# A decode block on one core: x stationary in the q projection and FFN up, h turned on VectorE, and other pieces for the last load

## The chip, the cores and the metric

The kernel runs on one core of one Trainium2 chip. The metric is the device time of one execution in microseconds (us). The kernel before took 122.86 us (median of 3 runs, 122.75 to 123.06). The engines carry their names in the profile: PE is TensorE's matmuls, PEld its weight loads, DVE is VectorE, ACT is ScalarE, POOL is GpSimd, and SP is SyncE, which issues the DMAs.

## The reference, cut to what matters

Eight tokens (one per batch entry) go through a layer norm. Then 32 query heads attend over the last 1,024 entries of a cache with 8 KV heads, a gated FFN runs beside it, and the two are multiplied.

```python
xn = _layernorm(x)                                   # x: [8, 1, 512], bf16
q  = xn @ wq                                         # wq: [512, 4096]
k, v = k_cache[:, :, Sk-W:, :], v_cache[:, :, Sk-W:, :]   # [8, 8, 1024, 128] each, W = 1024
s  = softmax(q k^T * Dh**-0.5) v, heads joined, @ wo # wo: [4096, 512]
g  = silu((gelu(xn @ w_gate) * (xn @ w_up)) @ w_down)# [512, 1792], [512, 1792], [1792, 512]
out = x + s * g
```

Only eight rows of x meet every weight, so the work is mostly loading: 47.5 MB of weights and cache are read once.

## The kernel before

Everything is loaded by one queue (SP) in a fixed order, into a ring of ten buffers: wq, then K and V for 16 units of work, then the FFN weights, then wo in four pieces.

```python
wq_t = [load_rows(A_wq, KD, k, 2, "wq_t") for k in (0, 2)]
# ... cut: layer norm, constants, the loop over 16 units that loads K and V ...
wg_t = load_rows(B_w_gate, KD, 0, KD, "wg_t")
wu_t = load_rows(B_w_up, KD, 0, KD, "wu_t")
load_cache(A_v_cache, NU - 1, v_t, "v_t")
wd_t = load_rows(B_w_down, FJ, 0, FJ, "wd_t")
wo_t = [[load_rows(A_wo[: HT * Dh, :], WI, 0, WI, "wo_t")]]          # first half, 16 rows per partition
wo_t.append([load_rows(A_wo[HT * Dh :, :], WI, 0, 8, "wo_t")])       # second half: 8 rows ...
nc.sync.dma_start(out=xr[0:P:4, :], in_=...)                         # x once more, 8 KB
wo_t[1].append(load_rows(A_wo[HT * Dh :, :], WI, 8, 5, "wo_t"))      # ... 5 rows ...
wo_t[1].append(load_rows(A_wo[HT * Dh :, :], WI, 13, 3, "wo_t"))     # ... and 3 rows
```

In the q projection and in FFN up, the weights are the stationary operand (the one that is loaded into the matmul array first: for q the trace has 128 loads of 128x128, 104 ns each, beside the 128 matmuls) and the eight columns of x move past them:

```python
for h in range(Hq):                       # 32 heads x 4 = 128 matmuls of 8 columns
    for k in range(KD):
        nc.tensor.matmul(qT_ps[:, h, :], wq_t[k // 2][:, k % 2, h * Dh : (h + 1) * Dh],
                         xnT[:, k, :], start=(k == 0), stop=(k == KD - 1))
# ... cut ...
for w, wt in enumerate((wg_t, wu_t)):     # 2 x 14 x 4 = 112 matmuls of 8 columns
    for j in range(FJ):
        for k in range(KD):
            nc.tensor.matmul(gu_ps[:, w, j, :], wt[:, k, :].rearrange("p (m j) -> p j m", j=FJ)[:, j, :],
                             xnT[:, k, :], start=(k == 0), stop=(k == KD - 1))
# ... cut: GELU on [128, 14, 8]; the product lands as hT, already turned ...
```

The end of the kernel multiplies wo in the order in which its pieces land, four column tiles (quarters of the array, 32 columns each) at a time, then two VectorE operations and the store follow:

```python
for t in range(NT):
    i = 0
    for w in wo_t[t]:
        for r in range(w.shape[1]):
            for q in range(NQ):
                nc.tensor.matmul(s_ps[32 * q : 32 * (q + 1), :], oR[:, t, i, :], w[:, r, q * NW : (q + 1) * NW],
                                 start=(t == 0 and i == 0), stop=(t == NT - 1 and i == WI - 1),
                                 tile_position=(0, 32 * q))
            i += 1
nc.vector.tensor_tensor(out=tmp, in0=s_ps, in1=g_sb, op=ALU.mult)
nc.vector.tensor_tensor(out=out_sb, in0=tmp, in1=xr, op=ALU.add)
```

The softmax here doesn't subtract the row's maximum and nothing guards it: scores larger than these inputs give would overflow.

Of the kernel before, what the change touches and what calls it, by code (L numbers as in the profile page):

```python
# [7 lines left out]
ACT = mybir.ActivationFunctionType  # L8
ALU = mybir.AluOpType
AX = mybir.AxisListType  # L10
BF16 = mybir.dt.bfloat16
FP32 = mybir.dt.float32
# [5 lines left out]
def kernel(  # L18
# [13 lines left out]
    nc = tc.nc  # L32

    B, Sq, D = A_x.shape
    Hkv, Sk, Dh = A_k_cache.shape[1], A_k_cache.shape[2], A_k_cache.shape[3]
    Hq = A_wq.shape[1] // Dh
# [3 lines left out]
    F = B_w_gate.shape[1]  # L40
    P = nc.NUM_PARTITIONS
    KD = D // P
    FJ = F // P
    CS = 4
    NH = Hkv // CS
    HS = CS * rep
# [4 lines left out]
    CC = 2 * HS  # L51
    NQ = 4
    NW = D // NQ
    NT = 2
    HT = Hq // NT
    WI = HT * Dh // P
# [6 lines left out]
    pad = ctx.enter_context(tc.tile_pool(name="pad", bufs=1))  # L63
    ring = ctx.enter_context(tc.tile_pool(name="ring", bufs=10))
    consts = ctx.enter_context(tc.tile_pool(name="consts", bufs=1))
    kT_pool = ctx.enter_context(tc.tile_pool(name="kT_pool", bufs=8))
    p_pool = ctx.enter_context(tc.tile_pool(name="p_pool", bufs=3))
    small = ctx.enter_context(tc.tile_pool(name="small", bufs=2))
    ps_k = ctx.enter_context(tc.tile_pool(name="ps_k", bufs=3, space=bass.MemoryType.PSUM))
    ps_s = ctx.enter_context(tc.tile_pool(name="ps_s", bufs=2, space=bass.MemoryType.PSUM))  # L70
    ps_p = ctx.enter_context(tc.tile_pool(name="ps_p", bufs=1, space=bass.MemoryType.PSUM))
# [5 lines left out]
    def bank(pool, name, shape, dtype=FP32):  # L77
        return pool.tile(shape, dtype, name=name, tag=pool.name)
# [9 lines left out]
    def load_rows(src, rows, r0, n, name):  # L88

        t = ring.tile([P, n, src.shape[1]], BF16, name=name, tag="slot")  # L90
        nc.sync.dma_start(out=t, in_=src.rearrange("(p r) n -> p r n", r=rows)[:, r0 : r0 + n, :])  # L91
        return t
# [3 lines left out]
    def load_cache(cache, u, slots, name):  # L96
# [10 lines left out]
    wq_t = [load_rows(A_wq, KD, k, 2, "wq_t") for k in (0, 2)]  # L107
# [4 lines left out]
    ident = consts.tile([P, P], BF16, name="ident")  # L112
    nc.vector.memset(ident, 0.0)
    nc.gpsimd.affine_select(
        out=ident, in_=ident, compare_op=ALU.not_equal, fill=1.0,
# [15 lines left out]
        out=xhat, in0=x_sb, scalar1=mv[:, 0:1], scalar2=rstd[:, 0:1],  # L131
        op0=ALU.subtract, op1=ALU.mult,
    )
    xnT = consts.tile([P, KD, B], BF16, name="xnT")
    xnT_ps = bank(ps_o, "xnT_ps", [P, KD, B], BF16)
    for k in range(KD):
        nc.tensor.transpose(
# [1 line left out]
            xhat.rearrange("b (p k) -> b k p", k=KD)[:, k, :],  # L139
            ident[0:B, 0:B],  # L140
        )
    nc.vector.tensor_copy(out=xnT, in_=xnT_ps)


    sel4 = consts.tile([P, CS], FP32, name="sel4")
# [1 line left out]
        out=sel4, in_=ident.rearrange("p (a n) -> p n a", n=CS), axis=AX.X, op=ALU.add  # L147
# [24 lines left out]
    identf = consts.tile([P, P], FP32, name="identf")  # L172
    nc.vector.tensor_copy(out=identf, in_=ident)

    perm = consts.tile([P, 2, 2, Dh // 2], BF16, name="perm")
    nc.vector.tensor_copy(
        out=perm,
        in_=ident.rearrange("p (i r) -> p r i", r=2).unsqueeze(2).to_broadcast([P, 2, 2, Dh // 2]),
    )

    own2 = consts.tile([P, 2], FP32, name="own2")
    nc.vector.tensor_reduce(
        out=own2, in_=ident.rearrange("p (g c n) -> p c g n", c=2, n=HS), axis=AX.XY, op=ALU.add
# [5 lines left out]
        in_=ident.rearrange("p (a n) -> p n a", n=HS), axis=AX.X, op=ALU.add,  # L189
    )  # L190

    Q2 = consts.tile([P, 2, B, NH, 2, HS], BF16, name="Q2")
    nc.vector.memset(Q2, 0.0)
    ownm = consts.tile([P, HT, WM], BF16, name="ownm")
    nc.vector.tensor_copy(out=ownm, in_=own16.unsqueeze(2).to_broadcast([P, HT, WM]))
    hT = consts.tile([P, FJ, 32], BF16, name="hT")
    nc.vector.memset(hT, 0.0)
    oR = consts.tile([P, NT, WI, 32], BF16, name="oR")
    nc.gpsimd.memset(oR, 0.0)


    qT = consts.tile([P, B, Hq], BF16, name="qT")
    qT_ps = bank(ps_s, "qT_ps", [P, Hq, B])
    for h in range(Hq):
        for k in range(KD):
            nc.tensor.matmul(  # L206
                qT_ps[:, h, :],
                wq_t[k // 2][:, k % 2, h * Dh : (h + 1) * Dh],
                xnT[:, k, :],
                start=(k == 0),  # L210
                stop=(k == KD - 1),
            )
    nc.vector.tensor_copy(out=qT, in_=qT_ps.rearrange("p h b -> p b h"))  # L213
    qp_ps = bank(ps_s, "qp_ps", [P, 2, B * NH, HS])
    for r in range(2):
        nc.tensor.matmul(
            qp_ps[:, r, :, :].rearrange("p a n -> p (a n)"),
            perm[:, r, :, :].rearrange("p c i -> p (c i)"),
            qT.rearrange("p b h -> p (b h)"),
            start=True, stop=True,  # L220
        )
    for c in range(2):
        p0 = c * (P // 2)
        nc.vector.tensor_copy(
            out=Q2[p0 : p0 + P // 2].rearrange("p r b h c n -> p r (b h) c n")[:, :, :, c, :],
            in_=qp_ps[p0 : p0 + P // 2],
        )


# [18 lines left out]
    def scores(u):  # L248
        h, b = divmod(u, B)
        sc_ps = bank(ps_s, "sc_ps", [P, NPC * P])  # L250
        nc.tensor.matmul(  # L251
            sc_ps, maskL.rearrange("p a n j -> p (a n j)"), maskR.rearrange("p a n -> p (a n)"),
            start=True, stop=False, skip_group_check=True,
        )
        for r in range(2):
            for g in range(NG):
                nc.tensor.matmul(  # L257
                    sc_ps[CC * g : CC * (g + 1), :],
                    Q2[:, r, b, h, :, :].rearrange("p c n -> p (c n)"),
                    kTs[u, g][:, :, r],  # L260
                    start=False, stop=(r == 1), tile_position=(0, CC * g),
                    skip_group_check=True,
                )
        ps[u] = p_pool.tile([P, NPC, P], BF16, name="p_sb")
        xs[u] = p_pool.tile([P, 2 * Dh + 1], FP32, name="x_u")
        nc.scalar.activation(  # L266
            out=ps[u].rearrange("p c s -> p (c s)"), in_=sc_ps, func=ACT.Exp, scale=inv_sqrt_dh,
            accum_out=xs[u][:, 2 * Dh : 2 * Dh + 1],
        )
# [97 lines left out]
    nc.sync.dma_start(  # L367
        out=xr[0:P:4, :], in_=x_flat.rearrange("b (q n) -> q b n", n=NW)
    )
    wo_t[1].append(load_rows(A_wo[HT * Dh :, :], WI, 8, 5, "wo_t"))  # L370
    wo_t[1].append(load_rows(A_wo[HT * Dh :, :], WI, 13, 3, "wo_t"))
    gather(NU - 3)
    turn(NU - 2)
    scores(NU - 1)
    values(NU - 2)


    gu_ps = bank(ps_s, "gu_ps", [P, 2, FJ, B])
    for w, wt in enumerate((wg_t, wu_t)):
        for j in range(FJ):  # L380
            for k in range(KD):
                nc.tensor.matmul(  # L382
                    gu_ps[:, w, j, :],
                    wt[:, k, :].rearrange("p (m j) -> p j m", j=FJ)[:, j, :],
                    xnT[:, k, :],
                    start=(k == 0),
                    stop=(k == KD - 1),
                )
    zT = gu_ps[:, 0, :, :]
    uT = gu_ps[:, 1, :, :]  # L390
    z2 = consts.tile([P, FJ, B], FP32, name="z2")
    nc.scalar.activation(out=z2, in_=zT, func=ACT.Square)  # L392
    nc.vector.tensor_scalar(  # L393
        out=z2, in0=z2, scalar1=0.044715, scalar2=1.0, op0=ALU.mult, op1=ALU.add
    )
    u3 = consts.tile([P, FJ, B], FP32, name="u3")
    nc.vector.tensor_tensor(out=u3, in0=z2, in1=zT, op=ALU.mult)
    th = consts.tile([P, FJ, B], FP32, name="th")
    nc.scalar.activation(out=th, in_=u3, func=ACT.Tanh, scale=0.7978845608028654)
    nc.vector.tensor_scalar(  # L400
        out=th, in0=th, scalar1=0.5, scalar2=0.5, op0=ALU.mult, op1=ALU.add
    )
    nc.vector.tensor_tensor(out=u3, in0=th, in1=zT, op=ALU.mult)
    nc.vector.tensor_tensor(out=hT[:, :, 0:32:4], in0=u3, in1=uT, op=ALU.mult)

    gather(NU - 2)
    turn(NU - 1)
# [25 lines left out]
    for t in range(NT):  # L433
        i = 0
# [47 lines left out]
```

## Time and profile before

| What | Value | View |
|---|---|---|
| time | 122.86 us (span of the profiled run 120.8) | times, page |
| DMA share of the 16 engines, 3 to 105 us | 1.01, at 426 to 429 GB/s | windows |
| PE, DVE, ACT busy | 78%, 52%, 20% of the span | page |
| last piece of wo landed | 116.61 us | landing records |

The first fence shows lines of the profile's page for the kernel before: span, busy time of each engine with its count of instructions, then two rows of the picture in 40 slices (one digit is tenths of a slice of 3 us), then the DMA queues (packets, MB, share of 16 engines), and last the shares of the chain that ended last.

```profile
span 120.8 us, 2828 instructions
PE 93.8 (78%) x1214; PEld 65.2 (54%) x1214; DVE 63.2 (52%) x125; ACT 24.1 (20%) x54; POOL 1.4 (1%) x6
...
PEclk9999999999999999999999967999999965555555
DMA  3999999999999999999999999999999999999700
...
q1 hardware_dynamic: 5976, 47.47, 93.4%
q8 instruction: 9, 0.15, 0.4%
q14 instruction: 3, 0.02, 0.0%
...
DMA 67%; PE 22%; DVE 4%; SPq 2%; issue 1%
```

The DMA row is full from the second slice to slice 37. The PE row is high too, but the chain names DMA. The windows view of the same kernel tells it in numbers (columns: stretch, length, busy time of each engine with its instructions, granted PE clock, DMA share, GB/s):

```profile
3.00:40.00 37.00, 26.06 (x329) 19.74 (x329) 20.34 (x46) 6.67 (x14) 0.00 (x0) 1.00 1.01 426
40.00:80.00 40.00, 36.09 (x383) 22.45 (x382) 26.58 (x45) 9.60 (x23) 0.00 (x0) 0.96 1.01 426
80.00:105.00 25.00, 23.36 (x297) 17.05 (x299) 11.03 (x22) 6.24 (x15) 0.00 (x0) 0.86 1.01 429
105.00:113.00 8.00, 6.15 (x162) 4.51 (x158) 3.80 (x8) 0.28 (x1) 0.00 (x0) 0.50 0.98 413
113.00:116.00 3.00, 1.63 (x52) 1.24 (x45) 0.00 (x0) 0.00 (x0) 0.00 (x0) 0.50 0.43 166
```

The stream never pauses until 113 us (share 0.98 to 1.01). Then the last three microseconds move little: DMA share 0.43. So a faster compute phase in the middle cannot help, and the question is what happens after 113 us. The timeline of the kernel before shows the phases that the change touches and the end (columns: start and length in us, engine, line, operation, output and input, count, and in brackets how long the engine was idle just before it and what ended that):

```profile
94.57 3.52 PE L382 MATMUL gu_ps<-xnT,wg_t 128*128 128x8 bf16 x56
98.97 3.52 PE L382 MATMUL gu_ps<-xnT,wu_t 128*128 128x8 bf16 x56 [0.87 <-DMA wu_t<-in_B_w_up_dram]
...
110.80 1.90 PE L438 MATMUL s_ps<-wo_t,oR 128*32 128x128 bf16 x64
112.86 1.04 PE L438 MATMUL s_ps<-wo_t,oR 128*32 128x128 bf16 x32 [0.16 <-DMA wo_t<-in_A_wo_dram]
114.40 0.72 PE L438 MATMUL s_ps<-wo_t,oR 128*32 128x128 bf16 x20 [0.50 <-DMA wo_t<-in_A_wo_dram]
116.66 0.51 PE L438 MATMUL s_ps<-wo_t,oR 128*32 128x128 bf16 x12 [1.53 <-DMA wo_t<-in_A_wo_dram]
117.22 0.29 DVE L446 TENSOR_TENSOR tmp<-s_ps,g_sb 128x128 f32<-128x128 f32 x1 [5.47 <-PE s_ps L438]
117.67 0.29 DVE L448 TENSOR_TENSOR out_sb<-tmp,xr 128x128 bf16<-128x128 f32 x1 [0.16 <-DVE tmp L446]
117.99 0.62 SPq L449 DMA_DIRECT2D out_dram<-out_sb  x1
```

PE waits 1.53 us for the last three rows of wo, 384 KB, which at 426 GB/s are 0.9 us of stream. Something holds that piece. The trace also records each increment of a DMA's semaphore. For the last piece of wo in the kernel before these are (us):

```
113.51 113.60 113.75 113.79 113.81 113.86 | 114.24 | 114.84 114.94 115.07 115.11 115.15 115.19 115.22 115.25 | 116.61
```

There are 16 increments, as many as the page counts DMA engines, and the matmuls start at 116.66, 0.05 us after the last of them and 1.41 us after the fifteenth. I take each increment as one engine that has landed its share. That is a reading of the counts: the records don't name the engine. On that reading six engines were done by 113.86, 2.75 us before the last one, and fifteen by 115.25, 1.36 us before it.

What held the others is in the third part of the page: queues of kind "instruction". The trace's packet records give their times in the kernel before (16 KB packets took 0.88 to 0.97 us, 8 KB packets 0.31 to 0.34 us):

```
16 KB (q8):  18.73  32.71  43.29  57.00  69.44  82.95  96.91  104.22  114.32
8 KB (q14):  40.70  85.77  118.32
```

Set beside the landings, each of them shows. In the DMA that ended after the first one, one engine landed 1.3 us after the other fifteen (21.49 against 20.17 us). After two, two engines were late (36.12 and 36.38; the next 34.91). After the 8 KB packet at 40.70 three, after the one at 43.29 four, and by 75.5 us six, after six packets. The delay stayed: after the first packet one engine was again last by 1.31 us at 23.92, by 1.26 us at 26.35 and by 1.24 us at 31.22. A stream in which every engine has its equal share to bring and no pause to catch up (DMA share 1.01 from 3 to 105 us) would fit. At the end there are nine late engines and one slightly late one, ten for the ten packets up to 104.22. The eleventh, at 114.32, made no tenth late engine. It made one that was already late land another 1.36 us later, alone at 116.61. After it, the last four packets of that engine start at 115.27 and end at 116.21, when all the other engines had ended by 114.97.

### The profile page before, as it was taken

Reading aid. Unit: us, or ns where it says so; the run is one execution under the profiler, and the core shown is the slowest. Engines: PE = TensorE matmul, PEld = TensorE weight load, DVE = VectorE, ACT = ScalarE, POOL = GpSimd, SP = SyncE. Lnnn points to the kernel's source line nnn. Section 1 sums busy time; section 2 is a strip of 40 time slices with the busy share of each in tenths; the row PEclk is TensorE's granted clock in tenths of the full one; section 3 lists DMA queues with packets and bytes.
Section 4 is the critical chain, followed back from the end, with each engine's and each line's share of the span. In section 5 each row is a group of like instructions: output and inputs, shape, how many; then the busy total and the mean of one; then the engine's idle time right before and its main releaser. Section 6 shows DMA issues by size and latency. Waiting matters only on the chain.

```text
span 120.8 us, 2828 instructions
## 1 busy us (share of the span) xinstructions
PE 93.8 (78%) x1214; PEld 65.2 (54%) x1214; DVE 63.2 (52%) x125; ACT 24.1 (20%) x54; POOL 1.4 (1%) x6
## 2 busy tenths in 40 slices
PE   0000789999987989889889399999999979786720
PEld 0000779666655655565556266666666869365610
DVE  3750039687745757458557964677676100457010
ACT  4500000241232212412133012412413300300000
POOL 4000000000000000000000000000000000000000
PEclk9999999999999999999999967999999965555555
DMA  3999999999999999999999999999999999999700
GB/s 100 434 434 426 415 428 423 428 420 428 428 420 426 428 420 426 428 426 423 423 434 423 434 412 428 426 428 426 423 453 422 420 418 444 429 423 409 320 6 5
DMA packets 6004, 47.65 MB, mean 394 GB/s; under 512 B 736, under 2 KB 744, under 8 KB 1000
## 3 DMA queue, kind: packets, MB, share of 16 engines
q1 hardware_dynamic: 5976, 47.47, 93.4%
q8 instruction: 9, 0.15, 0.4%
q14 instruction: 3, 0.02, 0.0%
q10 hardware_dynamic: 16, 0.01, 0.0%
HBM read 47.46 MB, written 0.01 MB: 393 GB/s over the span
## 4 chain that ended last, share of the span: by engine, by line
DMA 67%; PE 22%; DVE 4%; SPq 2%; issue 1%
DMA k_t<-in_A_k_cache_dram 49%; DMA wo_t<-in_A_wo_dram 18%; PE kT_ps L240 10%; PE tot L298 3%; PE sc_ps L257 3%; PE x_ps L283 3%; DVE kT L242 2%; SPq L100 2%; PE sc_ps L251 1%; PE pT_ps L274 1%; SPq L91 1%; DVE o_sb L315 1%; PE s_ps L438 0%; PE r_ps L333 0%; DVE e L322 0%
## 5 line engine op out<-in xcount | busy, mean ns | idle before, releaser
L242 DVE COPY kT<-kT_ps 128x1024 bf16<-128x1024 bf16 x64 | 42.6, 688 | 23.1 <-PE kT_ps L240 21.8
L240 PE MATMUL kT_ps<-identf,k_t 128*128 128x128 f32 x256 | 40.4, 298 | 3.0 <-DMA k_t<-in_A_k_cache_dram 3.0
L240 PEld LDWEIGHTS kT_ps<-identf,k_t 128*128 128x128 f32 x256 | 30.2, 150 | 14.1 <-issue 9.8
L266 ACT ACTIVATE p_sb<-sc_ps 128x512 bf16<-128x512 f32 x16 | 9.6, 597 | 39.6 <-PE sc_ps L257 26.0
L276 ACT COPY pT<-pT_ps 128x512 bf16<-128x512 bf16 x16 | 9.4, 586 | 31.0 <-PE pT_ps L274 31.0
L298 PE MATMUL tot<-x_u,zsel 128*128 128x257 f32 x32 | 12.2, 467 | 2.6 <-DVE x_u L289 2.4
L283 PE MATMUL x_ps<-v_t,pT 128*32 128x256 bf16 x256 | 10.4, 284 | 0.7 <-ACT pT L276 0.7
L257 PE MATMUL sc_ps<-kT,Q 128*32 128x512 bf16 x128 | 10.6, 407 | 0.0
L206 PE MATMUL qT_ps<-xnT,wq_t 128*128 128x8 bf16 x128 | 3.7, 168 | 8.2 <-DMA wq_t<-in_A_wq_dram 8.2
L298 PEld LDWEIGHTS tot<-x_u,zsel 128*128 128x128 f32 x32 | 5.2, 204 | 6.3 <-DVE x_u L289 6.3
L289 DVE TENSOR_TENSOR x_u<-x_ps,own 128x256 f32<-128x256 f32 x16 | 6.8, 422 | 2.8 <-PE x_ps L283 2.8
L206 PEld LDWEIGHTS <-wq_t 128*128 128x128 bf16 x128 | 3.6, 104 | 8.4 <-DMA wq_t<-in_A_wq_dram 8.4
L283 PEld LDWEIGHTS <-pT 128*32 128x32 bf16 x256 | 5.5, 98 | 4.2 <-issue 2.2
L251 PE MATMUL sc_ps<-maskR,maskL 128*128 128x512 bf16 x16 | 6.5, 405 | 0.0
L274 PE MATMUL pT_ps<-ident,p_sb 128*128 128x128 bf16 x64 | 6.4, 225 | 0.0
L274 PEld LDWEIGHTS <-p_sb 128*128 128x128 bf16 x64 | 5.0, 101 | 2.3 <-issue 0.3
L438 PE MATMUL s_ps<-wo_t,oR 128*32 128x128 bf16 x128 | 4.2, 310 | 2.2 <-DMA wo_t<-in_A_wo_dram 2.2
L257 PEld LDWEIGHTS <-Q 128*32 128x32 bf16 x128 | 1.9, 95 | 5.5 <-issue 5.5
L213 DVE CAST qT<-qT_ps 128x256 bf16<-128x256 f32 x1 | 0.4, 424 | 8.5 <-PE qT_ps L206 8.5
L438 PEld LDWEIGHTS <-oR 128*32 128x32 bf16 x128 | 3.3, 140 | 2.8 <-issue 2.8
L393 DVE TENSOR_SCALAR z<-z 128x112 f32<-128x112 f32 x1 | 0.2, 219 | 7.6 <-ACT z L392 7.6
L382 PE MATMUL gu_ps<-xnT,wu_t 128*128 128x8 bf16 x56 | 3.5, 202 | 0.9 <-DMA wu_t<-in_B_w_up_dram 0.9
(62 smaller groups left out, 42.6 us busy)
## 6 DMA issues: line engine op xcount, KB each, us to landing
k_t<-in_A_k_cache_dram SPq DMA_DIRECT2D x16, 1024.0 KB, 19.6
v_t<-in_A_v_cache_dram SPq DMA_DIRECT2D x16, 1024.0 KB, 19.7
wq_t<-in_A_wq_dram SPq DMA_DIRECT2D x2, 2048.0 KB, 9.4
wo_t<-in_A_wo_dram SPq DMA_DIRECT2D x1, 2048.0 KB, 27.4
wg_t<-in_B_w_gate_dram SPq DMA_DIRECT2D x1, 1792.0 KB, 21.4
wu_t<-in_B_w_up_dram SPq DMA_DIRECT2D x1, 1792.0 KB
wd_t<-in_B_w_down_dram SPq DMA_DIRECT2D x1, 1792.0 KB, 25.0
wo_t<-in_A_wo_dram SPq DMA_DIRECT2D x1, 1024.0 KB, 27.3
```

Of the source, the lines that this page charges most:

```text
L206: nc.tensor.matmul(qT_ps[:, h, :], wq_t[k // 2][:, k % 2, h * Dh : (h + 1) * Dh], xnT[:, k, :], start=(k == 0), stop=(k == KD - 1),)
L240: nc.tensor.transpose(kT_ps[:, pc, :], k32[:, w * P : (w + 1) * P], identf)
L242: nc.vector.tensor_copy(out=kT.rearrange("p s r -> p (s r)"), in_=kT_ps.rearrange("p c s -> p (c s)").bitcast(BF16),)
L251: nc.tensor.matmul(sc_ps, maskL.rearrange("p a n j -> p (a n j)"), maskR.rearrange("p a n -> p (a n)"), start=True, stop=False, skip_group ...
L257: nc.tensor.matmul(sc_ps[CC * g : CC * (g + 1), :], Q2[:, r, b, h, :, :].rearrange("p c n -> p (c n)"), kTs[u, g][:, :, r], start=False, s ...
L266: nc.scalar.activation(out=ps[u].rearrange("p c s -> p (c s)"), in_=sc_ps, func=ACT.Exp, scale=inv_sqrt_dh, accum_out=xs[u][:, 2 * Dh : 2 ...
L274: nc.tensor.transpose(pT_ps[:, pc, :], ps[u][:, pc, :], ident)
L276: nc.scalar.copy(out=pTs[u], in_=pT_ps)
L283: nc.tensor.matmul(x_ps[CC * g : CC * (g + 1), :, :].rearrange("p c d -> p (c d)"), pTs[u][:, pc, CC * g : CC * (g + 1)], v_t[u // 2][:, u ...
L289: nc.vector.tensor_tensor(out=xs[u][:, 0 : 2 * Dh].rearrange("p (c d) -> p c d", d=Dh), in0=x_ps, in1=own2.unsqueeze(2).to_broadcast([P, 2 ...
L298: nc.tensor.matmul(tot[h], zsel[:, B - 1 - b : P + B - 1 - b], xs[u], start=(b == 0), stop=(b == B - 1),)
L438: nc.tensor.matmul(s_ps[32 * q : 32 * (q + 1), :], oR[:, t, i, :], w[:, r, q * NW : (q + 1) * NW], start=(t == 0 and i == 0), stop=(t == N ...
```

## The change

The intent: PE does fewer and longer matmuls in the q projection and in FFN up (x, spread over 32 columns, is now the operand that is loaded, into each of four column tiles, and the weights move past it, up to 512 columns at once); the gate gets its own tile so that GELU can start before w_up lands; and the last load is cut smaller, so that less work is left when it lands. The price: q and h come out in rows and have to be turned, q by 16 small matmuls, h by one 32x32-block transpose on VectorE. Two of eight kT buffers are given up for the room.

```diff
-    kT_pool = ctx.enter_context(tc.tile_pool(name="kT_pool", bufs=8))
+    kT_pool = ctx.enter_context(tc.tile_pool(name="kT_pool", bufs=6))
...
+    xnT = consts.tile([P, KD, 32], BF16, name="xnT")
+    nc.vector.memset(xnT, 0.0)
...
-    for h in range(Hq):
-        for k in range(KD):
+    q_ps = [bank(ps_s, "q_ps", [P, HQ // 2, Dh]) for _ in range(2)]
+    for k in range(KD):
+        for s in range(2):
+            for t in range(NQ):
+                c0 = (t * HQ + s * HQ // 2) * Dh
+                nc.tensor.matmul(
+                    q_ps[s][32 * t : 32 * (t + 1), :, :].rearrange("p n d -> p (n d)"),
+                    xnT[:, k, :],
+                    wq_t[k // 2][:, k % 2, c0 : c0 + HQ // 2 * Dh],
+                    start=(k == 0), stop=(k == KD - 1), tile_position=(0, 32 * t),
+                )
... (four copies to q_row, then 16 matmuls with the identity turn q; Q2 is laid out with the batch innermost)
-    wo_t[1].append(load_rows(A_wo[HT * Dh :, :], WI, 8, 5, "wo_t"))
-    wo_t[1].append(load_rows(A_wo[HT * Dh :, :], WI, 13, 3, "wo_t"))
+    wo_t[1].append(load_rows(A_wo[HT * Dh :, :], WI, 8, 4, "wo_t"))
+    wo_t[1].append(load_rows(A_wo[HT * Dh :, :], WI, 12, 3, "wo_t"))
+    wo_t[1].append(load_rows(A_wo[HT * Dh :, :], WI, 15, 1, "wo_t"))
...
+    gu_ps = [bank(ps_s, "gu_ps", [P, FW]) for _ in range(2)]
     for w, wt in enumerate((wg_t, wu_t)):
-        for j in range(FJ):
-            for k in range(KD):
+        for k in range(KD):
+            for q in range(NQ):
                 nc.tensor.matmul(
+                    gu_ps[w][32 * q : 32 * (q + 1), :], xnT[:, k, :], wt[:, k, q * FW : (q + 1) * FW],
+                    start=(k == 0), stop=(k == KD - 1), tile_position=(0, 32 * q),
                 )
... (GELU on [128, 448] instead of [128, 112])
+    h_row = consts.tile([P, FJ, 32], BF16, name="h_row")
+    nc.vector.tensor_tensor(
+        out=h_row.rearrange("p j m -> p m j"),
+        in0=th.rearrange("p (m j) -> p m j", j=FJ),
+        in1=gu_ps[1].rearrange("p (m j) -> p m j", j=FJ), op=ALU.mult,
+    )
+    nc.vector.transpose(
+        out=hT.rearrange("p j b -> p (j b)"), in_=h_row.rearrange("p j m -> p (j m)")
+    )
```

The built program of PE falls from 2,455 to 2,131 instructions.

More of the change, by code (lines that the diff above doesn't have):

```diff
@@ L53 @@
     NW = D // NQ
+    FW = F // NQ
+    HQ = Hq // NQ
     NT = 2
@@ L133 @@
     )
-    xnT = consts.tile([P, KD, B], BF16, name="xnT")
+    xnT = consts.tile([P, KD, 32], BF16, name="xnT")
+    nc.vector.memset(xnT, 0.0)
     xnT_ps = bank(ps_o, "xnT_ps", [P, KD, B], BF16)
@@ L141 @@
         )
-    nc.vector.tensor_copy(out=xnT, in_=xnT_ps)
+    nc.vector.tensor_copy(out=xnT[:, :, 0:32:4], in_=xnT_ps)
     sel4 = consts.tile([P, CS], FP32, name="sel4")
@@ L173 @@
     nc.vector.tensor_copy(out=identf, in_=ident)
-    perm = consts.tile([P, 2, 2, Dh // 2], BF16, name="perm")
-    nc.vector.tensor_copy(
-        out=perm,
-        in_=ident.rearrange("p (i r) -> p r i", r=2).unsqueeze(2).to_broadcast([P, 2, 2, Dh // 2]),
-    )
     own2 = consts.tile([P, 2], FP32, name="own2")
@@ L190 @@
     )
-    Q2 = consts.tile([P, 2, B, NH, 2, HS], BF16, name="Q2")
+    Q2 = consts.tile([P, 2, NH, 2, HS, B], BF16, name="Q2")
     nc.vector.memset(Q2, 0.0)
@@ L195 @@
     nc.vector.tensor_copy(out=ownm, in_=own16.unsqueeze(2).to_broadcast([P, HT, WM]))
-    hT = consts.tile([P, FJ, 32], BF16, name="hT")
-    nc.vector.memset(hT, 0.0)
     oR = consts.tile([P, NT, WI, 32], BF16, name="oR")
     nc.gpsimd.memset(oR, 0.0)
-    qT = consts.tile([P, B, Hq], BF16, name="qT")
-    qT_ps = bank(ps_s, "qT_ps", [P, Hq, B])
-    for h in range(Hq):
-        for k in range(KD):
-            nc.tensor.matmul(
-                qT_ps[:, h, :],
-                wq_t[k // 2][:, k % 2, h * Dh : (h + 1) * Dh],
-                xnT[:, k, :],
-                start=(k == 0),
-                stop=(k == KD - 1),
-            )
@@ L213 @@
-    nc.vector.tensor_copy(out=qT, in_=qT_ps.rearrange("p h b -> p b h"))
-    qp_ps = bank(ps_s, "qp_ps", [P, 2, B * NH, HS])
-    for r in range(2):
-        nc.tensor.matmul(
-            qp_ps[:, r, :, :].rearrange("p a n -> p (a n)"),
-            perm[:, r, :, :].rearrange("p c i -> p (c i)"),
-            qT.rearrange("p b h -> p (b h)"),
-            start=True, stop=True,
-        )
+    q_ps = [bank(ps_s, "q_ps", [P, HQ // 2, Dh]) for _ in range(2)]
[9 more added lines that the diff above has]
+                )
@@ new lines @@
+    q_row = consts.tile([P, HQ, 2, 2, Dh // 2], BF16, name="q_row")
+    for s in range(2):
+        for r in range(2):
+            q_out = q_row[:, s * HQ // 2 : (s + 1) * HQ // 2, r, :, :]
+            q_in = (
+                q_ps[s].rearrange("p n (i r) -> p r n i", r=2)[:, r, :, :]
+                .unsqueeze(2).to_broadcast([P, HQ // 2, 2, Dh // 2])
+            )
+            if r == 0:
+                nc.vector.tensor_copy(out=q_out, in_=q_in)
+            else:
+                nc.scalar.copy(out=q_out, in_=q_in)
@@ L222 @@
+    qp_ps = bank(ps_p, "qp_ps", [P, 2, NQ, HQ, B])
+    for n in range(HQ):
+        for r in range(2):
+            nc.tensor.matmul(
+                qp_ps[:, r, :, n, :],
+                q_row[:, n, r, :, :].rearrange("p c i -> p (c i)"),
+                ident[:, 0:P:4].rearrange("p (t b) -> p t b", b=B),
+                start=True, stop=True,
+            )
     for c in range(2):
@@ L224 @@
         nc.vector.tensor_copy(
-            out=Q2[p0 : p0 + P // 2].rearrange("p r b h c n -> p r (b h) c n")[:, :, :, c, :],
-            in_=qp_ps[p0 : p0 + P // 2],
+            out=Q2[p0 : p0 + P // 2, :, :, c, :, :].rearrange("p r h n b -> p (r h) (n b)"),
+            in_=qp_ps[p0 : p0 + P // 2].rearrange("p r (h t) n b -> p (r h) (t n b)", h=NH),
         )
@@ L258, in scores @@
                     sc_ps[CC * g : CC * (g + 1), :],
-                    Q2[:, r, b, h, :, :].rearrange("p c n -> p (c n)"),
+                    Q2[:, r, h, :, :, b].rearrange("p c n -> p (c n)"),
                     kTs[u, g][:, :, r],
@@ L375 @@
     values(NU - 2)
-    gu_ps = bank(ps_s, "gu_ps", [P, 2, FJ, B])
+    gu_ps = [bank(ps_s, "gu_ps", [P, FW]) for _ in range(2)]
     for w, wt in enumerate((wg_t, wu_t)):
-        for j in range(FJ):
-            for k in range(KD):
+        for k in range(KD):
+            for q in range(NQ):
                 nc.tensor.matmul(
-                    gu_ps[:, w, j, :],
-                    wt[:, k, :].rearrange("p (m j) -> p j m", j=FJ)[:, j, :],
+                    gu_ps[w][32 * q : 32 * (q + 1), :],
                     xnT[:, k, :],
-                    start=(k == 0),
-                    stop=(k == KD - 1),
-                )
-    zT = gu_ps[:, 0, :, :]
-    uT = gu_ps[:, 1, :, :]
-    z2 = consts.tile([P, FJ, B], FP32, name="z2")
-    nc.scalar.activation(out=z2, in_=zT, func=ACT.Square)
+                    wt[:, k, q * FW : (q + 1) * FW],
+                    start=(k == 0), stop=(k == KD - 1), tile_position=(0, 32 * q),
+                )
+    z2 = consts.tile([P, FW], FP32, name="z2")
+    nc.scalar.activation(out=z2, in_=gu_ps[0], func=ACT.Square)
     nc.vector.tensor_scalar(
@@ L395 @@
     )
-    u3 = consts.tile([P, FJ, B], FP32, name="u3")
-    nc.vector.tensor_tensor(out=u3, in0=z2, in1=zT, op=ALU.mult)
-    th = consts.tile([P, FJ, B], FP32, name="th")
-    nc.scalar.activation(out=th, in_=u3, func=ACT.Tanh, scale=0.7978845608028654)
+    nc.vector.tensor_tensor(out=z2, in0=z2, in1=gu_ps[0], op=ALU.mult)
+    th = consts.tile([P, FW], FP32, name="th")
+    nc.scalar.activation(out=th, in_=z2, func=ACT.Tanh, scale=0.7978845608028654)
     nc.vector.tensor_scalar(
@@ L402 @@
     )
-    nc.vector.tensor_tensor(out=u3, in0=th, in1=zT, op=ALU.mult)
-    nc.vector.tensor_tensor(out=hT[:, :, 0:32:4], in0=u3, in1=uT, op=ALU.mult)
+    nc.vector.tensor_tensor(out=th, in0=th, in1=gu_ps[0], op=ALU.mult)
+    h_row = consts.tile([P, FJ, 32], BF16, name="h_row")
[4 more added lines that the diff above has]
+    )
+    hT = consts.tile([P, FJ, 32], BF16, name="hT")
+    nc.vector.transpose(
+        out=hT.rearrange("p j b -> p (j b)"), in_=h_row.rearrange("p j m -> p (j m)")
+    )
     gather(NU - 2)
```

## The prediction

> **What bounds the kernel now.** The load stream. In the busy-tenths view the DMA row is full from slice 2 to slice 37; the windows view reads 425 to 432 GB/s and a DMA share of about 1.0 from 3 to 105 us, for 47.5 MB. PE (78%) and DVE (52%) have slack; the DMA queue's own waits are nearly all for earlier DMAs. So faster q and FFN-up are worth nothing by themselves; only the end counts: in the chain of waits the last piece of wo (3 rows) lands at 116.61 us, then 12 matmuls (0.51), two DVE operations and a store.
>
> **Why that landing is late.** The trace's landing records of the last piece show 16 engines' increments: six at 113.5 to 113.9, one at 114.24, eight at 114.8 to 115.25, one alone at 116.61. [...] The packet records show what held the engines: an instruction queue moved nine 16 KB packets (879 to 967 ns each) during the run, and two of 8 KB. After each, one more engine lands about 1.0 to 1.4 us later for good (0.4 after the second 8 KB one). The ninth, at 114.32, hit an engine already behind, and its last four packets trail to 116.21. [...]
>
> **What the change does.**
> - PE: 1,214 matmul and weight-load pairs become 1,052 (q 128 to 32, the turn of q 2 to 16, FFN up 112 to 32); 2,131 PE instructions in all. I expect eight 16 KB fetches instead of nine, so no engine is hit twice: last landing about 115.25. **-1.35 us, on the path.**
> - wo pieces 5+3 become 4+3+1: packets took 196 ns (5 KB) and 121 ns (3 KB); 1 KB packets took 44; eight of each per engine makes +0.07 us on the stream (estimate). After the landing 4 matmuls remain instead of 12, though the 3-row piece lands only about 0.4 us earlier and its 12 matmuls (0.51) are hardly done. Net **-0.1 to -0.2 us**.
> - Off the path: q ready about 1 us earlier; FFN up 3.5 us per matrix to about 1 to 2; the GELU works on 448 elements per partition instead of 112 (0.22 to 0.40 us operations become perhaps 0.4 to 0.7), but the gate's part now overlaps the wait for w_up, since gate and up have separate tiles. The turn of h adds perhaps 0.6. Regroup should come near 108.5 to 109.5 instead of 110.28, before wo's first half lands (110.32).
> - Six kT buffers suffice: PE order frees them in time.
>
> **Predicted: 121.3 us, range 120.8 to 122.2.** Faster by over 2%: 0.06; within 2%: 0.92; slower: 0.02.
>
> **Right if** packets show eight 16 KB fetches, the last landing is near 115.3, no engine stands alone a microsecond behind, the last DVE multiply starts near 115.7, and DMA stays full from 3 to 113 us.
>
> **Wrong if** the last fetch still hits an already late engine (then about 122.6); the strided q weights or 1 KB packets are slow; or the longer DVE work delays regroup past 110.3 so PE reaches the last pieces late (then little is gained).

The sum: 122.86 us before, less 1.35 for the landing, less 0.1 to 0.2 for the smaller pieces, is 121.3 to 121.4. The expected count of eight fetches is an estimate from the kernel before: nine 16 KB packets for 2,455 PE instructions are 7.8 for 2,131. That these packets fetch PE's program was a reading as well; the experiments support it, as the ninth packet moves with the number of PE instructions (at 114.32 us with 2,455, at 111.66 with 2,527 in e9, none with 2,131). The times off the path are estimates. The trace of the kernel before has numbers of their size (128 matmuls of 512 columns on L257 busy for 10.6 us, so 1.3 us for 16; DVE casts of 512 elements in 688 ns on L224 and of 256 in 424 ns on L213). None of them enters the sum.

## The result, and the profile after

The changed kernel took 121.6 us (median of 4 runs, 121.41 to 121.69). The ratio to the kernel before is 0.9892, with a 95% interval of 0.9874 to 0.9911. Here and below a ratio is the mean time of one kernel's fast runs over the mean of the other's, so it is not quite the ratio of the medians that are quoted. A ratio to before always takes the runs of before on the same chip (median 123.03, 123.01 and 122.97 us in the three groups of experiments).

The same lines of the page for the changed kernel:

```profile
span 119.5 us, 2515 instructions
PE 88.9 (74%) x1052; PEld 58.5 (49%) x1052; DVE 67.1 (56%) x126; ACT 25.8 (22%) x56; POOL 1.4 (1%) x6
...
PEclk9999999999999999999999967999999998555596
DMA  4999999999999999999999999999999999999920
...
q1 hardware_dynamic: 6120, 47.47, 94.6%
q8 instruction: 8, 0.13, 0.4%
q14 instruction: 3, 0.02, 0.0%
...
DMA 85%; PE 5%; DVE 4%; SPq 2%; issue 1%
```

The same bytes, the same full DMA row, eight packets instead of nine in q8. The windows view of the changed kernel says that the stream runs as it did:

```profile
3.00:40.00 37.00, 26.86 (x251) 18.16 (x251) 21.14 (x47) 7.85 (x16) 0.00 (x0) 1.00 1.01 426
40.00:80.00 40.00, 36.23 (x380) 23.39 (x380) 26.31 (x45) 9.61 (x23) 0.00 (x0) 0.96 1.01 425
80.00:105.00 25.00, 19.78 (x227) 11.85 (x226) 15.57 (x27) 6.81 (x15) 0.00 (x0) 0.91 1.02 431
105.00:113.00 8.00, 4.11 (x136) 3.73 (x136) 2.65 (x5) 0.28 (x1) 0.00 (x0) 0.50 0.98 412
113.00:116.00 3.00, 1.95 (x64) 1.41 (x63) 0.00 (x0) 0.00 (x0) 0.00 (x0) 0.83 0.44 167
```

From 113 us on it still moves little (share 0.44 against 0.43): the engines still end up to 2 us apart. Only the clock that PE was granted differs there, 0.83 against 0.50; what that is worth is said further down.

The timeline of the changed kernel, FFN up, the turn of h and the end:

```profile
94.73 0.93 PE L394 MATMUL gu_ps<-wg_t,xnT 128*32 128x448 bf16 x16
...
98.81 0.94 PE L394 MATMUL gu_ps<-wu_t,xnT 128*32 128x448 bf16 x16 [3.15 <-DMA wu_t<-in_B_w_up_dram]
...
99.80 2.11 DVE L413 TENSOR_TENSOR h_row<-th,gu_ps 128x448 bf16<-128x448 f32 x1 [0.71 <-PE gu_ps L394]
...
101.95 0.64 DVE L420 STREAM_TRANSPOSE hT<-h_row 128x448 bf16<-128x448 bf16 x1
...
110.77 1.90 PE L456 MATMUL s_ps<-wo_t,oR 128*32 128x128 bf16 x64 [2.63 <-DMA wo_t<-in_A_wo_dram]
113.22 0.98 PE L456 MATMUL s_ps<-wo_t,oR 128*32 128x128 bf16 x32 [0.56 <-DMA wo_t<-in_A_wo_dram]
114.52 0.41 PE L456 MATMUL s_ps<-wo_t,oR 128*32 128x128 bf16 x16 [0.31 <-DMA wo_t<-in_A_wo_dram]
115.44 0.56 PE L456 MATMUL s_ps<-wo_t,oR 128*32 128x128 bf16 x16 [0.52 <-DMA wo_t<-in_A_wo_dram]
116.05 0.29 DVE L464 TENSOR_TENSOR tmp<-s_ps,g_sb 128x128 f32<-128x128 f32 x1 [7.06 <-PE s_ps L456]
...
116.69 0.62 SPq L467 DMA_DIRECT2D out_dram<-out_sb  x1
```

FFN up fell from 3.52 to 0.93 us for each matrix, and nearly all of that turned into waiting: PE now stands idle 3.15 us for w_up and 2.63 us for the first half of wo, where before it waited 0.87 us for w_up and not at all for wo's first half. The end of the path is what moved:

| Stretch of the end (us) | before | after | difference |
|---|---|---|---|
| last piece of wo landed, at | 116.61 | 115.72 | -0.89 |
| from there to the first DVE operation | 0.61 | 0.33 | -0.28 |
| from there to the issue of the store | 0.77 | 0.64 | -0.13 |
| from there to the end of the span | 2.85 | 2.78 | -0.07 |

The instruction packets and the landings of the last piece in the changed kernel:

```
16 KB (q8):  27.34  38.21  52.29  66.94  78.60  92.04  105.42  113.54
8 KB (q14):  38.84  85.61  103.51  121.34
landings:    113.61 113.67 113.73 113.82 113.89 113.90 113.99 | 114.43 | 115.16 115.17 115.19 115.22 115.24 115.25 115.26 | 115.72
```

The ninth 16 KB packet is gone, and with it the engine at 116.61. A third 8 KB packet has moved in, from 118.32 to 103.51, and in this execution one engine is 0.46 us behind its neighbours.

The landing records of the DMAs before it show two things more. First, that third 8 KB packet fell on an engine that was already late. In the DMA that ended at 101.20, one of the late engines stood apart at 100.64, before six others at 101.09 to 101.20. In the next DMA, the first to end after the packet, its place (about 104.9) is empty, and a new last engine stands at 105.89, 0.46 us after the next. In e7 and e12, two runs below without the packet, that place stays filled (104.78 and 104.84). Second, the eighth 16 KB packet, at 113.54, delayed nobody: eight engines were more than a microsecond late before it, and eight after it. That fits a packet on one of the seven engines that were just then ending (they landed from 113.61 on), but the records don't name the engine.

### The profile page after: what moved, and what is told of

It is laid out like the page before. It is cut to its first block, busy times and chain, and to the rows that moved or that the text cites. A ratio compares the mean times of both kernels' runs of the same rounds, so it can differ in the third digit from the quotient of the medians.

```text
span 119.5 us, 2515 instructions
## 1 busy us (share of the span) xinstructions
PE 88.9 (74%) x1052; PEld 58.5 (49%) x1052; DVE 67.1 (56%) x126; ACT 25.8 (22%) x56; POOL 1.4 (1%) x6
## 4 chain that ended last, share of the span: by engine, by line
DMA 85%; PE 5%; DVE 4%; SPq 2%; issue 1%
DMA k_t<-in_A_k_cache_dram 50%; DMA wg_t<-in_B_w_gate_dram 18%; DMA wo_t<-in_A_wo_dram 17%; PE kT_ps L250 2%; DVE kT L252 2%; SPq L102 2%; SPq L93 1%; DVE o_sb L325 1%; PE tot L308 1%; PE s_ps L456 0%; PE sc_ps L267 0%; PE pT_ps L284 0%; DVE e L332 0%; PE sc_ps L261 0%; PE r_ps L343 0%
## 5 line engine op out<-in xcount | busy, mean ns | idle before, releaser
L250 PEld LDWEIGHTS kT_ps<-identf,k_t 128*128 128x128 f32 x256 | 30.4, 152 | 13.6 <-issue 10.6
L308 PE MATMUL tot<-x_u,zsel 128*128 128x257 f32 x32 | 11.7, 450 | 2.6 <-DVE x_u L299 2.4
L267 PE MATMUL sc_ps<-kT,Q 128*32 128x512 bf16 x128 | 11.2, 426 | 0.0
L204 PE MATMUL q_ps<-wq_t,xnT 128*32 128x512 bf16 x32 | 3.8, 626 | 6.4 <-DMA wq_t<-in_A_wq_dram 6.4
L267 PEld LDWEIGHTS <-Q 128*32 128x32 bf16 x128 | 3.3, 147 | 5.4 <-issue 5.4
L204 PEld LDWEIGHTS <-xnT 128*32 128x32 bf16 x32 | 1.2, 129 | 8.1 <-issue 7.7
L220 DVE CAST q_row<-q_ps 128x512 bf16<-128x512 f32 x2 | 1.3, 688 | 6.8 <-PE q_ps L204 6.8
L222 ACT CAST q_row<-q_ps 128x512 bf16<-128x512 f32 x2 | 1.2, 586 | 11.5 <-DVE q_row L220 11.5
```

Of the source, the lines that this page charges most:

```text
L204: nc.tensor.matmul(q_ps[s][32 * t : 32 * (t + 1), :, :].rearrange("p n d -> p (n d)"), xnT[:, k, :], wq_t[k // 2][:, k % 2, c0 : c0 + HQ / ...
L250: nc.tensor.transpose(kT_ps[:, pc, :], k32[:, w * P : (w + 1) * P], identf)
L267: nc.tensor.matmul(sc_ps[CC * g : CC * (g + 1), :], Q2[:, r, h, :, :, b].rearrange("p c n -> p (c n)"), kTs[u, g][:, :, r], start=False, s ...
L308: nc.tensor.matmul(tot[h], zsel[:, B - 1 - b : P + B - 1 - b], xs[u], start=(b == 0), stop=(b == B - 1),)
```

## The experiments

The theory under test, called the fetch theory: what the change gains is that one fetch of instructions no longer falls into the load stream onto an engine that is already late. Rival A: the smaller last piece of wo is what gains. Rival B: the faster PE phases are what gains. There were twelve runs, all correct, in three groups of four (the first two groups on one chip, the third on another); landings are those of each run's one profiled execution.

### One part alone

**e1_split_only**: the kernel before with only the pieces of wo changed.

```diff
-    wo_t[1].append(load_rows(A_wo[HT * Dh :, :], WI, 8, 5, "wo_t"))
-    wo_t[1].append(load_rows(A_wo[HT * Dh :, :], WI, 13, 3, "wo_t"))
+    wo_t[1].append(load_rows(A_wo[HT * Dh :, :], WI, 8, 4, "wo_t"))
+    wo_t[1].append(load_rows(A_wo[HT * Dh :, :], WI, 12, 3, "wo_t"))
+    wo_t[1].append(load_rows(A_wo[HT * Dh :, :], WI, 15, 1, "wo_t"))
```

Expected:

> The kernel before with only the last pieces of wo changed (8, 5, 3 rows become 8, 4, 3, 1). Fetch theory: the PE program keeps its 2,455 instructions, so nine 16 KB instruction fetches stay in the stream, the ninth again hits an engine that is already behind, and the last landing stays at 116.6 to 116.8 us with one engine about 1.3 us behind the rest; only the shorter end after the landing helps, so 0.1 to 0.4 us faster than before (about 122.6, ratio 0.997 to 0.999). Rival A, the split is what gains: about 121.6, ratio 0.989. Rival B, the faster q and FFN up are what gains: no difference from before.

Measured: 122.89 us, ratio 0.9984 (0.9971 to 0.9997). Nine 16 KB fetches, the ninth at 114.44; last landing 116.84, alone, the next at 115.38. So the smaller pieces are worth 0.2 us (0.0016 of 123; the interval is 0.04 to 0.36 us), not the gain. Rival A falls.

**e2_no_split**: the changed kernel with the old pieces.

```diff
-    wo_t[1].append(load_rows(A_wo[HT * Dh :, :], WI, 8, 4, "wo_t"))
-    wo_t[1].append(load_rows(A_wo[HT * Dh :, :], WI, 12, 3, "wo_t"))
-    wo_t[1].append(load_rows(A_wo[HT * Dh :, :], WI, 15, 1, "wo_t"))
+    wo_t[1].append(load_rows(A_wo[HT * Dh :, :], WI, 8, 5, "wo_t"))
+    wo_t[1].append(load_rows(A_wo[HT * Dh :, :], WI, 13, 3, "wo_t"))
```

> The changed kernel with the last pieces of wo back at 8, 5, 3 rows. Fetch theory: eight 16 KB fetches, last landing 115.2 to 115.8 us, 12 matmuls after it; 121.4 to 122.0 (ratio to before 0.988 to 0.993). If the third 8 KB fetch (at 103.5 us in the changed kernel, after the end of the stream in the kernel before) belongs to the SP queue, which now has one DMA fewer, it goes back to the end and the last landing is near 115.25; if it belongs to DVE it stays in the stream and one engine lands about 0.45 us after the rest. Rival A (split): back to about 122.9. Rival B (faster PE phases): 121.6, as changed.

Measured: 121.72 us, ratio 0.9888 (0.9873 to 0.9904), eight 16 KB fetches, last landing 115.65. The gain is there without the split. It doesn't come from the PE clock either: the mean granted clock of this profiled execution is 0.880, against 0.891 before. The third 8 KB fetch stayed in the stream, at 103.47, though SP had one DMA fewer, while in e1 (200 instructions on DVE, 79 on SP) it came at 118.28. So it goes with the DVE program and not with SP's.

**e3_q_only**: the kernel before with only the q projection changed, and six kT buffers (those that hold turned K). The cut below is against the changed kernel; the pieces of wo are as before.

```diff
     (q projection, xnT 32 wide, Q2 layout, kT_pool bufs=6: as in the change)
-    gu_ps = [bank(ps_s, "gu_ps", [P, FW]) for _ in range(2)]   (FFN up, GELU, hT: as before)
+    gu_ps = bank(ps_s, "gu_ps", [P, 2, FJ, B])
...
+                    xnT[:, k, 0:32:4],
```

> The kernel before with only the q projection changed (x stationary, six kT buffers); FFN up and the pieces of wo as before. PE program 2,291 instructions. Fetch theory: the ninth 16 KB fetch comes at the very end of the PE program, after the stream, or not at all, so no engine is hit twice: last landing 115.2 to 115.8, about 121.4 to 122.1, so this half of the change alone gives nearly the whole gain of about 1.2 us (ratio 0.988 to 0.994). Rival B (each faster PE phase pays for itself): q ends about 0.8 us earlier at 18 us but the stream hides it, FFN up is as before, so nothing or at most half of the gain (122.3 to 122.9). Rival A (split): 122.9.

Measured: 121.76 us, ratio 0.9895 (0.988 to 0.9909). The ninth 16 KB fetch came at 115.93, after the last data packet (115.39). Last landing 115.75.

**e4_up_only**: the kernel before with only FFN up and the turn of h changed, and six kT buffers. The cut is against the kernel before.

```diff
     (FFN up, GELU on [P, FW], h_row and the transpose, xnT 32 wide, kT_pool bufs=6: as in the change)
     for h in range(Hq):
         for k in range(KD):
...
-                xnT[:, k, :],
+                xnT[:, k, 0:32:4],
```

> The kernel before with only FFN up and the turn of h changed (six kT buffers); q and the pieces of wo as before. PE program 2,295 instructions. Fetch theory: as for q alone, the ninth 16 KB fetch falls after the stream, last landing 115.2 to 115.8, about 121.4 to 122.1 (ratio 0.988 to 0.994): the two halves do not add up, either one gives all. Rival B: the gain is here, because PE reaches the end earlier: 121.6 too, but then q alone gives nothing. Rival A (split): 122.9.

Measured: 121.79 us, ratio 0.9895 (0.9882 to 0.9909). The ninth fetch came at 116.20, after the last data packet (115.35). Last landing 115.68.

The two halves do not add up: either gives the whole gain. In e3, FFN up is as slow as before and PE reaches wo's first half no earlier (110.86 us, against 110.80 before); in e4, q is as before. What they share is a PE program of 2,291 or 2,295 instructions, and an end of the stream that the ninth fetch misses. They also share the six kT buffers and the x spread over 32 columns, so these two runs alone leave open that one of those is what gains; e9 below, which has both and loses most of the gain, rules that out. The end of e3 in its timeline:

```profile
110.86 1.90 PE L451 MATMUL s_ps<-wo_t,oR 128*32 128x128 bf16 x64
...
115.80 0.35 PE L451 MATMUL s_ps<-wo_t,oR 128*32 128x128 bf16 x12 [0.46 <-DMA wo_t<-in_A_wo_dram]
116.19 0.29 DVE L459 TENSOR_TENSOR tmp<-s_ps,g_sb 128x128 f32<-128x128 f32 x1 [4.39 <-PE s_ps L451]
```

Rival B falls too: the last 12 matmuls of e3 start at 115.80, not at 116.66, with PE no faster on the way there.

### Putting the fetch back

These take the whole change and add PE instructions that do nothing, in the three long waits of PE, so that nothing but the length of the program should differ:

```diff
+def pad(n):   # written out at: after k == 1 of the q projection, after the gate's matmuls, before s_ps
+    dm = bank(ps_k, "dm", [P, 8])
+    for i in range(n):
+        nc.tensor.matmul(dm[32 * (i % NQ) : 32 * (i % NQ) + 32, :], ident[:, 0:32], ident[:, 0:8],
+                         start=True, stop=True, tile_position=(0, 32 * (i % NQ)))
```

**e5_pad_162** (n = 54):

> The changed kernel with 162 small matmuls added (128x32 weights, 8 columns, into an unread PSUM tile), 54 each in three waits of PE (before the second half of wq, before w_up, before the first half of wo): the PE program is back at 2,455 instructions and nothing else differs. Fetch theory: a ninth 16 KB fetch again falls into the stream at about 113 to 115 us and hits an engine that is already behind; last landing 116.3 to 116.9, about 122.4 to 122.9, so nearly the whole gain is lost (ratio to before 0.995 to 1.000) although q, FFN up and the pieces are as changed. Rivals A (split) and B (faster PE phases): 121.6 to 121.8, as changed, since the added work sits in waits.

Measured: 121.36 us, ratio 0.9857 (0.984 to 0.9873). The expectation failed: nothing was lost. The ninth fetch was there, but at 115.11 us instead of 114.32, when the last data packet of any engine was to end at 115.25. Last landing 115.57, nobody alone. The theory does not say that the number of fetches matters, but where they fall; I had taken the same distance from the program's end for the same time. This run alone would not have decided anything.

**e6_pad_81** (n = 27):

> As the run with 162 added matmuls, but 27 in each place, 81 in all: 2,293 PE instructions, as many as with q alone or FFN up alone. Fetch theory: the ninth fetch falls after the end of the stream (after 115.4 us), so no loss: 121.5 to 121.9 (ratio 0.988 to 0.992). If the added matmuls cost time by themselves, half of the loss of the other run shows here.

Measured: 121.47 us, ratio 0.9861 (0.9842 to 0.9881); ninth fetch at 115.54, last landing 115.59. The added matmuls by themselves cost nothing that shows (the changed kernel has ratios of 0.9892 and 0.9881).

**e9_pad_198** (n = 66), to bring the ninth fetch well inside:

> As the run with 162 added matmuls, but 66 in each of the three waits, 198 in all, 2,527 PE instructions. In the run with 162 the ninth 16 KB fetch came at 115.11 us, when the engines had almost finished, and cost nothing; here the same point of the program comes 72 instructions earlier from its end, before the wait for wo's first half. Fetch theory: the ninth fetch falls at about 111 to 113.5 us, inside the stream, onto an engine that an earlier fetch has already delayed; one engine lands about 1.3 us behind the rest, last landing 116.4 to 117.0, about 122.3 to 122.9 (ratio to before 0.994 to 1.000). If the fetches are not what sets the end, this stays at 121.3 to 121.7 as the runs with 81 and 162.

Measured: 122.59 us, ratio 0.9969 (0.9955 to 0.9983), against 121.48 and 0.9881 of the changed kernel in the same rounds (e11): 1.1 us lost. The ninth fetch came at 111.66. Landings of the last piece:

```
113.67 113.70 113.71 113.88 113.89 113.97 | 114.91 | 115.11 115.13 115.20 115.21 115.24 115.28 115.31 115.50 | 116.61
```

One engine is alone again, 1.1 us behind the next, as in the kernel before. The landing records show it being hit: in the DMA that landed before the fetch, the last engine came at 110.50, 0.17 us after the next; in the one that landed after it, at 114.14, 1.19 us after the next, and the number of late engines stayed at ten. (A tenth fetch came at 116.42, after the last data packet.) The timeline of e9 shows the wait for it, already at the 8 rows (1.74 us where the changed kernel has 0.56):

```profile
110.54 1.90 PE L476 MATMUL s_ps<-wo_t,oR 128*32 128x128 bf16 x64 [2.02 <-DMA wo_t<-in_A_wo_dram]
114.18 1.04 PE L476 MATMUL s_ps<-wo_t,oR 128*32 128x128 bf16 x32 [1.74 <-DMA wo_t<-in_A_wo_dram]
...
116.33 0.62 PE L476 MATMUL s_ps<-wo_t,oR 128*32 128x128 bf16 x16 [0.32 <-DMA wo_t<-in_A_wo_dram]
```

PE had done its own work in time: the 64 matmuls of wo's first half start at 110.54, earlier than in the changed kernel. With e6 (fewer such matmuls, no loss) and e5 (nearly as many, fetch too late to matter) this settles the cause: a fetch that falls into the stream onto a late engine.

**e10_pad_321** (n = 107), to see whether two such fetches cost twice:

> As before, 107 in each wait, 321 added matmuls, 2,773 PE instructions: nine and ten fetches fall inside the stream. Fetch theory: the tenth hits another engine than the ninth, so two engines are behind by two fetches instead of one, and the end is the same as with 198: last landing 116.4 to 117.1, 122.3 to 122.9. If each fetch beyond eight costs its own 1.3 us, about 124; if nothing, 121.4 to 121.8.

Measured: 123.0 us, ratio 1.0005 (0.9986 to 1.0023), just above the range that the theory had given. Last landing 116.67, one engine alone, the next at 115.64. But the tenth fetch came only at 114.98, when its engine, whichever it was, could hardly be held any more, so the question whether two cost twice stays open. The rest of the loss is something else. In the timeline of e10 PE stands still where no data is missing:

```profile
107.98 0.97 PE L466 MATMUL dm<-ident 128*32 128x8 bf16 x101
...
112.25 0.22 PE L466 MATMUL dm<-ident 128*32 128x8 bf16 x6 [3.29 <-issue]
...
116.40 0.51 PE L476 MATMUL s_ps<-wo_t,oR 128*32 128x128 bf16 x10 [0.32 <-DMA wo_t<-in_A_wo_dram]
117.35 0.40 PE L476 MATMUL s_ps<-wo_t,oR 128*32 128x128 bf16 x6 [0.44 <-issue]
```

"issue" means that the profile shows nothing that PE waited for. It stops in the middle of a row of 107 equal matmuls whose operands have long been there, and it stops again six matmuls before the end, after the tenth fetch. That PE had run out of fetched instructions fits, since the ninth fetch came at 109.91 and the tenth at 114.98, but no run isolates it.

### The third 8 KB fetch, and the slow product

**e7_dve_200**: setup work moved from DVE to POOL, until DVE has 200 instructions again.

```diff
-    nc.vector.memset(xr, 0.0)
+    nc.gpsimd.memset(xr, 0.0)
     (the same for ident, eps_sb, xnT, zsel and Q2, and for the copy to identf)
```

> The changed kernel with six memsets and one copy of the setup moved from DVE to POOL, so that DVE has 200 instructions instead of 207, as the kernel before. Fetch theory: the third 8 KB fetch, at 103.5 us in the changed kernel, goes back behind the end of the stream (about 117 us or later); the engine that landed 0.45 us after the rest falls back among them: last landing about 115.25, 121.1 to 121.4 (ratio to before 0.984 to 0.987, and 0.3 to 0.5 us under the changed kernel). Rival: the late engine has another cause, or POOL's memsets delay the start: 121.6 or more.

Measured: 121.37 us, ratio 0.9861 (0.9847 to 0.9876). The fetch moved as expected, to 116.88, and the last landing was 115.44, with no engine alone. Whether that is time gained over the changed kernel this group cannot say, because the changed kernel was not in it; the runs with added matmuls on the same chip, which keep the fetch at 103 us, took as long (e5, e6). The landing of about 115.25 that was expected did not come.

**e8_hrow_order**: the product that writes h_row, in the order of its output.

```diff
-        out=h_row.rearrange("p j m -> p m j"),
-        in0=th.rearrange("p (m j) -> p m j", j=FJ),
-        in1=gu_ps[1].rearrange("p (m j) -> p m j", j=FJ), op=ALU.mult,
+        out=h_row,
+        in0=th.rearrange("p (m j) -> p j m", j=FJ),
+        in1=gu_ps[1].rearrange("p (m j) -> p j m", j=FJ), op=ALU.mult,
```

> The changed kernel with the product that writes h in rows walked in the order of its output, so that it writes neighbouring elements and reads at a step of 14 elements, where the changed kernel writes at a step of 32 elements. If the step of the writes is what made this operation take 2.11 us for 448 elements, it now takes 0.6 to 0.7 us, as the other products of 448 elements (0.62); if the step of the reads costs as much, it stays near 2. The whole time does not move in either case (121.4 to 121.8), because PE waits for w_down after it.

Measured: 121.58 us in its single run, and the product took 0.92 us instead of 2.11:

```profile
100.06 0.92 DVE L413 TENSOR_TENSOR h_row<-th,gu_ps 128x448 bf16<-128x448 f32 x1 [0.83 <-PE gu_ps L394]
```

So it was the writes at a step of 32 bf16 elements that cost; the reads at a step of 14 fp32 elements cost 0.30 us over the 0.62 us of the other products of this size. For the 448 elements of the slow product, 2.11 us are 4.7 ns each. And 1.2 us less on DVE moved nothing, because w_down lands after that in any case (PE waited for it until 105.83 us in this run).

**e11_after_again**: the changed kernel, unaltered, beside the third group.

> The changed kernel once more, unaltered, on this chip beside the others: 121.3 to 121.7, ratio to before 0.986 to 0.989. It is the base for the added matmuls and for the last version.

Measured: 121.48 us, ratio 0.9881 (0.9866 to 0.9896). Last landing 115.54, the next at 115.43: the lone engine of the first profile (0.46 us behind) is not there in this execution, with the third 8 KB fetch at 102.82.

**e12_dve_200_hrow**: e7 and e8 together, the candidate for a better version.

> The changed kernel with both small edits: setup memsets on POOL so that DVE has 200 instructions, and h written in the order of its output. Fetch theory: third 8 KB fetch after the stream, last landing 115.2 to 115.5; 0.1 to 0.4 us under the changed kernel of the same rounds (121.0 to 121.4). The shorter product (0.92 instead of 2.11 us) adds nothing, as PE waits for w_down after it. If the third 8 KB fetch costs nothing, equal to the changed kernel within 0.1 us.

Measured: 121.48 us, ratio 0.988 (0.9866 to 0.9893), the same as e11. The third 8 KB fetch is out of the stream (116.92), and the last landing is 115.42 against 115.54. The expected gain of 0.1 to 0.4 us did not appear. The profiles show where the tenth of a microsecond went: the two last DVE operations of e12 stand 0.15 us apart, and those of e11 follow each other at once, so that the store is issued at 116.57 against 116.52. That gap of 0.15 to 0.16 us is in all four kernels with 200 DVE instructions (before, e1, e7, e12) and in none of the other ten profiles, which have 206 or 207; no run shows why. No version beats the changed kernel clearly.

## Why the prediction was right

- **The bound.** That the load stream is the bound and that faster PE phases are worth nothing by themselves held: 3.52 us became 0.93 us twice, and PE waited longer for w_up (3.15 against 0.87 us). e3 shows it from the other side: PE at wo's first half no earlier, and yet the whole gain.
- **The cause of the late landing.** The ninth 16 KB fetch onto a late engine: predicted from the landing and packet records of the kernel before, shown by e3 and e4 (either half moves it out, either gives all) and by e9 (put back, 1.1 us lost). The prediction argued with the number of fetches, and that is not what decides: e3, e4, e5 and e6 have nine and lose nothing, because the ninth comes when the engines have nothing, or next to nothing, left to bring.
- **Its size.** Predicted: last landing about 115.25, worth 1.35 us, and 0.07 us more for smaller packets. Measured: 115.72 in the first profile, 115.54 in e11, so 0.9 to 1.07 us. The term was mis-sized by some 0.2 to 0.4 us (against 115.32, with the 0.07), and the prediction's mark for the last multiply, 115.7, was missed by as much (116.05). I had not counted that seven more DVE instructions would bring a third 8 KB fetch into the stream, and "no engine is hit twice" did not hold to the letter: that fetch hit a late engine. Without it (e7, e12) the last landing was 115.44 and 115.42, so 0.1 to 0.3 us of the difference is its doing; the other 0.1 us stays open.
- **The smaller pieces.** Predicted 0.1 to 0.2 us net. The end after the landing shortened by 0.28 us to the first DVE operation, and e1 gives 0.2 us for the whole of it. A part of the 0.28 is the clock that PE was granted at the end, 0.50 in the profile before and 1.00 after. Two runs whose matmuls took as long as those at 0.50 compare better: e2 with the old pieces (its last 12 matmuls took 0.51 us, as before) needs 0.60 us from the landing to that operation, and e5 with the new ones (16 matmuls in 0.62 us, as at 115.40 in e9, where the clock was 0.50 from 113 to 116 us) needs 0.38, so the pieces give 0.22. Right, and a small part. In the changed kernel two pieces feed one row of 16 matmuls without a pause (115.44 to 116.00), because the last row lands 0.32 us after the three before it.
- **Off the path.** Regroup came at 107.55 us, still earlier than the 108.5 to 109.5 predicted, and waited for wo's first half (110.77) as expected. "Perhaps 0.4 to 0.7 us" for the operations on 448 elements held for all but one: the product that writes h_row took 2.11 us. The kernel before had the clue. In the groups by line of that kernel, two operations on 128 elements stand together, one that writes neighbouring elements (L311) and one that writes at a step of 8 elements (L315):

```profile
L315 DVE SCALAR_TENSOR_TENSOR o_sb<-tot,rcp,o_f 128x128 bf16<-128x128 f32 x2 | 1.6, 808 | 0.1
...
L311 DVE TENSOR_SCALAR o_f<-tot,rcp 128x128 f32<-128x128 f32 x2 | 0.7, 351 | 0.1
```

  808 ns against 351 for as many elements is 3.6 ns more for each. (L315 also reads a second tensor; L446 does too and takes 291 ns, so that is not the cost.) For 448 elements that is an estimate of 1.6 us on top of the 0.62 of a plain product, 2.2 in all. It cost nothing here because w_down landed at 105.9 us, well after hT was ready.
- **The total.** 121.3 predicted, 121.6 and 121.48 measured, within the range of 120.8 to 122.2. The mis-sized landing took back 0.2 to 0.4 us; a shorter path from the first DVE operation to the store (0.13 us, the gap that goes with 200 DVE instructions, see e12), which I had not predicted, gave a little. That the total was missed by no more than 0.2 to 0.3 us owes a little to this, which was luck.

## What to carry to other kernels

In a kernel that is bound by one unbroken load stream, look at what else uses the same DMA engines (here the instruction packets: after one of 0.88 to 0.97 us, one more engine was about 1.0 to 1.4 us late for the rest of the kernel), and at when each engine's last share lands, not only at when the transfer is complete: one engine alone behind the rest was 1.1 to 1.4 us here that faster compute by itself did not give back. The length of the instruction program was part of that here, even on an engine that was not the bottleneck (nine 16 KB packets for 2,455 PE instructions, eight for 2,131; the ninth put back into the stream in e9 cost 1.1 us), and fewer, longer instructions can pay in this way where their own speed pays nothing. But it pays by where a fetch falls and not by the count of fetches, so read the fetches from the packet records before counting on it, and again afterwards.
